# Moving the second head's normalisation of 16 steps from ScalarE to GpSimd in an attention and gated feed-forward kernel

## The chip, the cores and the metric

The kernel runs on one core of a Trainium2 chip. The metric is the time of one execution on the device in microseconds; less is better. A core has five engines that work side by side and wait for each other by semaphores: TensorE (PE in the profile, with PEld for its weight loads), VectorE (DVE), ScalarE (ACT), GpSimd (POOL) and SyncE (SP), whose queue issues most DMAs. TensorE multiplies from SBUF into PSUM. Each engine runs its own instructions strictly in order.

## The reference, cut to what matters

Four batches, eight heads, 768 positions, head width 64. Attention looks back over 96 positions and at 8 global keys, with a distance bias by head; its output goes through a feed-forward part with a convolution of three taps and a gate.

```python
scores = q @ k.T / 8 - slope[h] * dist
scores = where(keep, scores, -1e9)
scores = scores - scores.max(-1)
a = exp(scores)
a = a / (a.sum(-1) + 1e-9)
x = a @ v
h = maximum(x @ w_in, 0)
c = conv3(h, conv_w)
out = (h * sigmoid(c)) @ w_out
```

Changed is who carries out the division in the fifth line, for one of every two heads and for 16 of 96 steps.

## The kernel before, in words

Attention is cut into 32 pairs of heads (4 batches, 2 halves of the sequence, 4 pairs of heads), and each pair into 3 blocks of 128 query rows. One block of one pair is a **step**; there are 96, numbered from 0. For step s, whose pair is m = s // 3, these functions run, each for both heads (j = 0 and 1):

- `scores(s)`, L372: TensorE multiplies queries by the 232 keys in reach (136 for the first block of a sequence), tiles `s` (and `sb`, the second head's, in the first 27 steps). The PSUM tile for the scores has two buffers, so step s + 2 cannot be scored before the exponentials of step s have read theirs.
- `maxima(s)`, L404: VectorE adds the bias table and takes the row's extreme, one instruction a head (L412), into `mm`.
- `exps(s)`, L419: ScalarE takes the exponential with the row sum (L426) into `pbuf`, of which there are three. Below step 32 ScalarE also adds the 1e-9 to both sums (L432).
- `normalise(s)`, L434: VectorE takes the reciprocal of the sums (L438); from step 32 on it first adds the 1e-9 itself (L437). Then each head's exponentials are multiplied by the reciprocal: the first head's by GpSimd (L444), the second head's by ScalarE below step 32 (L442) and by GpSimd from there on.
- `transposes(s)` and `evict(s)`: TensorE transposes `pbuf` into `t` (L452, four matmuls a step), ScalarE copies it out as `pt` (L457).
- After the third step of a pair, `values(m)` multiplies by v into `pv` (L473, 24 matmul rows of the trace a pair), which has one buffer. ScalarE copies it to `xh` (L485), VectorE takes the remainder `xl` = pv - xh (L489). Only then can the next pair's values be written.

The feed-forward part of every half sequence is cut into small items: `mm1` (L507, tiles `h`), `relu` on ScalarE (L517), `conv` (first tap on ScalarE, L555, for the first two halves, then on GpSimd, L557; the other two on VectorE, L558 and L559, tile `c`), the gate (L577), `split` (L610 to L613, tiles `gh` and `gl`) and `mm2` (L622, tile `o`). They are queued and drawn from between the steps. Weights arrive as 64-bit numbers; VectorE takes each piece apart in three instructions (L316, L318, L320, tile `w`), GpSimd makes the high part (L325), VectorE the remainder (L331, tile `wol`). From pair 9 on GpSimd also copies keys and queries (`prep`, L137 and L138, tiles `kk` and `qh`), and VectorE takes their remainders (L141, and L142 into `ql`).

The order on each engine up to step 15 is that of the code. From `HAND = 16` on a scheduler orders all instructions of all engines from its own estimates of their lengths, and so it places every later instruction anew when one instruction changes its engine. `SHARED` is 32.

```python
        if s < HAND:
            scores(s)
...
                normalise(s - 1)
...
        else:
            if hand:
                hand = False
                cur["auto"] = True
                manual.__exit__(None, None, None)
```

Of the kernel before, what the change touches and what calls it, by code (L numbers as in the profile page):

```python
# [36 lines left out]
SHARED = 32  # L37
CHECK_EVERY = 3
HAND = 16
# [28 lines left out]
def fast_path(tc, io):  # L68
# [365 lines left out]
    def normalise(s):  # L434
        pb, c0, n, mm = st_s[s]
        if s >= SHARED:
            V.tensor_scalar(mm[:, 4:6], mm[:, 2:4], 1.0e-9, None, ALU.add)  # L437
        V.reciprocal(mm[:, 6:8], mm[:, 4:6])  # L438
        for j in range(2):
            x, inv = pb[:, j, c0 : c0 + n], mm[:, 6 + j : 7 + j]  # L440
            if j and s < SHARED:
                A.activation(x, x, AF.Copy, scale=inv)  # L442
            else:
                G.tensor_scalar(x, x, inv, 1.0, ALU.mult, ALU.mult)  # L444
# [340 lines left out]
    for s in range(len(steps) + LAG_V + 1):  # L785
        cur["s"] = s
        m, i = steps[s] if s < len(steps) else (len(jobs), -1)
        if s < HAND:
# [14 lines left out]
            if s:  # L803
                normalise(s - 1)
# [17 lines left out]
        else:  # L822
# [20 lines left out]
            if s <= len(steps):  # L843
                normalise(s - 1)
# [222 lines left out]
```

## Time and profile before

| | us |
|---|---|
| median of 3 runs | 446.5 |
| fastest and slowest of them | 445.61 and 447.54 |
| the profiled execution, its own time | 445.31 |
| its span in the profile | 443.5 |
| TensorE busy in the span | 431.2 |
| VectorE busy | 357.2 |
| ScalarE busy | 309.9 |
| GpSimd busy | 221.2 |

The span runs from the first instruction to the last. Durations are of one execution on the hardware; stretches are given in us from the span's start. A mean length stands in ns, times in us. The granted clock is TensorE's, as a share of full speed. Matmuls overlap in the pipeline, so a single matmul's length is longer than the distance to the next. A wait names the instruction that ended it. Step 16 begins at about 43 us, and steps 16 to 31 are normalised until about 108 us.

### The profile page before, as it was taken

What the parts mean: (1) busy time and instruction counts of PE and PEld (TensorE: products, weight loads), DVE (VectorE), ACT (ScalarE), POOL (GpSimd) and SP (SyncE); (2) the same over time, 40 slices, a digit from 0 to 9 for tenths busy, and PEclk for the clock granted to TensorE, in tenths of its full rate; (3) what the DMA queues carried; (4) which work ended last, traced back from release to release, by engine and by line L of the source; (5) the groups of instructions that cost most, each with busy time, mean ns of one, the idle gap of its engine ahead of it and who ended that gap; (6) DMA issues with size and microseconds to landing.
All of it is one profiled execution on the core that took longest, in us unless ns stands there. A gap on an engine that the chain in (4) does not pass through costs nothing.

```text
span 443.5 us, 9050 instructions
## 1 busy us (share of the span) xinstructions
PE 431.2 (97%) x3039; PEld 374.5 (84%) x3039; DVE 357.2 (81%) x935; ACT 309.9 (70%) x839; POOL 221.2 (50%) x307
## 2 busy tenths in 40 slices
PE   8988999799999999999999999999999999999996
PEld 7655778799889988899889988899988998798876
DVE  6899899998999988757998989747999975568700
ACT  4889988789896678546876865665776776755540
POOL 5555334654456786556757744647656841013000
PEclk9999999899999999999999999999999999999999
DMA  6998953141543244442246134423235313980111
GB/s 210 294 255 258 271 184 110 40 163 65 153 128 120 75 136 132 128 125 94 85 128 192 41 107 145 141 102 104 67 119 181 103 48 122 312 295 32 47 49 55
DMA packets 22662, 60.02 MB, mean 135 GB/s; under 512 B 3024, under 2 KB 5584, under 8 KB 22608
## 3 DMA queue, kind: packets, MB, share of 16 engines
q1 hardware_dynamic: 18992, 53.01, 39.2%
q10 hardware_dynamic: 3616, 6.36, 3.9%
q8 instruction: 26, 0.43, 0.4%
q14 instruction: 28, 0.23, 0.2%
HBM read 53.07 MB, written 6.29 MB: 134 GB/s over the span
## 4 chain that ended last, share of the span: by engine, by line
PE 81%; DVE 8%; DMA 6%; ACT 3%; issue 1%; POOL 0%; SPq 0%; DVEq 0%; ACTq 0%
PE o L622 26%; PE h L507 25%; PE pv L473 10%; PE t L452 9%; PE s L395 7%; DMA check<-in_w 3%; PE s L385 1%; PE last L643 1%; DMA out<-ob 1%; DVE w L320 1%; DVE w L318 1%; ACT junkb L350 1%; ACT pbuf L426 1%; DMA rq<-in_qk 1%; PE sb L385 1%
## 5 line engine op out<-in xcount | busy, mean ns | idle before, releaser
L444 POOL TENSOR_SCALAR pbuf<-pbuf,mm 128x232 f32<-128x232 f32 (+1 forms) x160 | 113.3, 718 | 81.0 <-DVE mm L438 49.5
L426 ACT ACTIVATE pbuf<-s,mm 128x232 f32<-128x232 f32 (+1 forms) x165 | 72.1, 442 | 48.3 <-DVE mm L412 34.6
L412 DVE CUSTOM_DVE_ANT_0 s<-s,tab 128x232 f32<-128x232 f32 (+1 forms) x165 | 63.1, 385 | 20.2 <-PE s L395 15.7
L622 PE MATMUL o<-woh,gh 128*128 128x512 f32 x184 | 74.1, 403 | 0.0
L622 PE MATMUL o<-woh,gl 128*128 128x512 f32 x184 | 73.5, 400 | 0.0
L622 PE MATMUL o<-wol,gh 128*128 128x512 f32 x184 | 73.3, 398 | 0.0
L452 PE MATMUL t<-ident,pbuf 128*128 128x128 f32 x384 | 65.4, 279 | 5.4 <-ACT pbuf L442 2.7
L557 POOL TENSOR_SCALAR c<-hbuf,cw 128x382 f32<-128x382 f32 (+1 forms) x48 | 38.6, 807 | 56.5 <-ACT hbuf L517 56.5
L452 PEld LDWEIGHTS t<-ident,pbuf 128*128 128x128 f32 x384 | 46.4, 141 | 20.2 <-ACT pbuf L442 6.4
L457 ACT ACTIVATE pt<-t 128x512 f32<-128x512 f32 x96 | 57.0, 597 | 8.3 <-PE t L452 8.0
L507 PE MATMUL h<-xl,wih 128*128 128x384 f32 x252 | 59.4, 343 | 0.0
L507 PE MATMUL h<-xh,wih 128*128 128x384 f32 x252 | 58.8, 347 | 0.1
L507 PE MATMUL h<-xh,wil 128*128 128x384 f32 x252 | 55.8, 339 | 0.0
L473 PE MATMUL pv<-pt,v 128*64 128x128 f32 (+1 forms) x768 | 50.3, 280 | 0.3 <-DVE xl L489 0.2
L473 PEld LDWEIGHTS pv<-pt,v 128*64 128x64 f32 (+1 forms) x768 | 42.5, 138 | 8.6 <-issue 3.6
L558 DVE SCALAR_TENSOR_TENSOR c<-hbuf,cw,c 128x382 f32<-128x382 f32 (+1 forms) x64 | 44.3, 699 | 4.8 <-POOL c L557 3.7
L559 DVE SCALAR_TENSOR_TENSOR c<-hbuf,cw,c 128x382 f32<-128x382 f32 (+1 forms) x64 | 45.4, 712 | 0.3
L507 PEld LDWEIGHTS h<-xh,wih 128*128 128x128 f32 x252 | 43.2, 190 | 2.1 <-ACT pbuf L426 0.9
L507 PEld LDWEIGHTS h<-xl,wih 128*128 128x128 f32 x252 | 43.9, 189 | 0.7 <-issue 0.7
L507 PEld LDWEIGHTS h<-xh,wil 128*128 128x128 f32 x252 | 44.1, 188 | 0.0
L517 ACT ACTIVATE hbuf<-h 128x384 f32<-128x384 f32 x64 | 31.4, 495 | 13.5 <-PE h L507 12.5
L622 PEld LDWEIGHTS o<-woh,gl 128*128 128x128 f32 x184 | 34.6, 188 | 7.3
(120 smaller groups left out, 856.1 us busy)
## 6 DMA issues: line engine op xcount, KB each, us to landing
v<-in_vv SPq DMA_DIRECT2D x32, 384.0 KB, 3.6
rq<-in_qk SPq DMA_DIRECT2D x23, 384.0 KB, 3.1
wr<-in_w SPq DMA_DIRECT2D x16, 512.0 KB, 5.3
check<-in_w SPq DMA_DIRECT2D x16, 512.0 KB, 4.9
rk<-in_qk SPq DMA_DIRECT2D x12, 504.0 KB, 3.6
out<-ob ACTq DMA_DIRECT2D x23, 256.0 KB, 2.4
rk<-in_qk SPq DMA_DIRECT2D x11, 408.0 KB, 3.6
rq<-in_qk SPq DMA_DIRECT2D x16, 96.0 KB, 5.1
```

The costliest lines, as they stand in the source:

```text
L412: last_ttr[s] = V.tensor_tensor_reduce(out=sp[j][:, c0 : c0 + n], in0=sp[j][:, c0 : c0 + n], in1=tb, scale=-0.125, scalar=3.0e38, op0=ALU. ...
L426: last_exp[s] = A.activation(pb[:, j, c0 : c0 + n], sp[j][:, c0 : c0 + n], AF.Exp, bias=mm[:, j : j + 1], scale=-1.0, accum_out=mm[:, 2 + ...
L444: G.tensor_scalar(x, x, inv, 1.0, ALU.mult, ALU.mult)
L452: T.transpose(pt[:, j, c, :], pb[:, j, c * P : (c + 1) * P], ident)
L457: last_ev[s] = A.activation(sb, st_pt[s], AF.Copy)
L473: T.matmul(pv[m][64 * j : 64 * j + 64, i * P : (i + 1) * P], vt[m][:n, i, c, 64 * j : 64 * j + 64], sb[:n, j, c, :], start=c == 0, stop=c ...
L507: T.matmul(ps[:, :TB], w_[:, k, fs], x_, start=part == 0 and k == 0, stop=part == 2 and k == NK - 1,)
L517: A.activation(half, ps[:, :TB], AF.Relu, scale=0.5)
L557: G.tensor_scalar(c, *tap(1), 1.0, ALU.mult, ALU.mult)
L558: V.scalar_tensor_tensor(c, *tap(0), c, ALU.mult, ALU.add)
L559: V.scalar_tensor_tensor(c, *tap(2), c, ALU.mult, ALU.add)
L622: last = T.matmul(ps, g_[:, f], w_[:, f], start=f == 0 and part == 0, stop=f == NF - 1 and part == 2,)
```

## The change

```diff
         for j in range(2):
             x, inv = pb[:, j, c0 : c0 + n], mm[:, 6 + j : 7 + j]
-            if j and s < SHARED:
+            if j and s < HAND:
                 A.activation(x, x, AF.Copy, scale=inv)
             else:
                 G.tensor_scalar(x, x, inv, 1.0, ALU.mult, ALU.mult)
```

For steps 16 to 31 the second head's exponentials are multiplied by GpSimd, like the first head's. ScalarE goes on adding the 1e-9 up to step 31, and VectorE from step 32 on. Steps 0 to 15 and 32 to 95 have the same instructions as before; from about 48 us on the scheduler orders them anew, until about 245 us.

On GpSimd, steps 16 to 20 (`mm` and the number behind it name the step; `woh` and `wih` are weight casts):

```order
 L325 CAST wih_186<-w3_1_748 128x512
 L444 TENSOR_SCALAR pbuf0_193<-pbuf0_193,mm15_774 128x232
-L444 TENSOR_SCALAR pbuf1_194<-pbuf1_194,mm16_807 128x232
+L444 TENSOR_SCALAR pbuf1_194<-pbuf1_194,mm16_807 128x232 x2
 L325 CAST woh_188<-w4_0_791 128x512
+L444 TENSOR_SCALAR pbuf2_195<-pbuf2_195,mm17_840 128x232 x2
 L325 CAST woh_188<-w4_1_873 128x512
-L444 TENSOR_SCALAR pbuf2_195<-pbuf2_195,mm17_840 128x232
-L444 TENSOR_SCALAR pbuf0_193<-pbuf0_193,mm18_880 128x232
-L444 TENSOR_SCALAR pbuf1_194<-pbuf1_194,mm19_939 128x232
+L444 TENSOR_SCALAR pbuf0_193<-pbuf0_193,mm18_880 128x232 x2
+L444 TENSOR_SCALAR pbuf1_194<-pbuf1_194,mm19_939 128x232 x2
```

Every step's normalisation is now two instructions in a row, and step 17's stands in front of a weight cast that it stood behind.

On VectorE, from step 27's second maximum to the remainder `xl` of pair 6, which the values of pair 7 wait for (`ISA` is the maximum; the row behind each reads its result out):

```order
-L558 SCALAR_TENSOR_TENSOR c0_865<-hbuf_190,cw_185,c0_865 128x382
 L412 ISA s27_1285,mm27_1290<-s27_1285,tab_166 128x136
 L412 ISA mm27_1290 128x1
+L316 TENSOR_SCALAR w7_1_1329<-wr7_1_1065 128x512
+L558 SCALAR_TENSOR_TENSOR c0_865<-hbuf_190,cw_185,c0_865 128x382
 L438 RECIPROCAL mm26_1261<-mm26_1261 128x2
-L316 TENSOR_SCALAR w7_1_1329<-wr7_1_1065 128x512
-L331 TENSOR_TENSOR wol_189<-w6_1_1199,woh_188 128x512
 L412 ISA s28_1342,mm28_1347<-s28_1342,tab_166 128x232
 L412 ISA mm28_1347 128x1
 L489 TENSOR_TENSOR xl6_1222<-pv6_1171,xh6_1221 128x384
```

The tap L558 has moved from in front of the maximum to behind it, and the weight remainder L331 from in front of `xl6` to behind it.

On VectorE, around step 40's maxima, which step 42's scores wait for:

```order
-L412 ISA s40_1963,mm40_1968<-s40_1963,tab_166 128x232
-L412 ISA mm40_1968 128x1
 L613 TENSOR_TENSOR gl0_4_1947<-hbuf_190,gh0_4_1946 128x1024
 L412 ISA s40_1963,mm40_1968<-s40_1963,tab_166 128x232
 L412 ISA mm40_1968 128x1
+L489 TENSOR_TENSOR xl11_1974<-pv11_1917,xh11_1973 128x384
 L437 TENSOR_SCALAR mm39_1908<-mm39_1908 128x2
+L412 ISA s40_1963,mm40_1968<-s40_1963,tab_166 128x232
+L412 ISA mm40_1968 128x1
 L412 ISA s41_2018,mm41_2023<-s41_2018,tab_166 128x232
```

The remainder `xl11` and the addition L437 now stand in front of step 40's second maximum; counted from the start, only L437 is new ahead of it, since `xl11` stood further forward before.

## Rows read from the trace of the kernel before

**Rows 1.** The waits, TensorE, 50 to 400 us: total us, times, longest us.

```profile
PE s L395 <- ACT pbuf L426: 2.1, 1, 2.1
PE pv L473 <- DVE xl L489: 0.2, 1, 0.2
```

**Rows 2.** Busy time by stretch, the columns in the first line.

```profile
core 0: us, PE busy (x) PEld busy (x) DVE busy (x) ACT busy (x) POOL busy (x), PEclk, DMA share, GB/s
...
70.00:80.00 10.00, 10.00 (x78) 8.95 (x77) 9.94 (x27) 9.72 (x32) 6.30 (x7) 1.00 0.39 122
80.00:90.00 10.00, 7.70 (x57) 6.87 (x57) 9.94 (x24) 7.13 (x21) 5.72 (x6) 0.83 0.24 72
90.00:140.00 50.00, 50.00 (x368) 45.48 (x368) 47.71 (x110) 43.34 (x110) 24.63 (x29) 1.00 0.40 126
...
45.00:107.00 62.00, 59.70 (x422) 51.76 (x422) 58.33 (x150) 54.02 (x159) 28.60 (x34) 0.97 0.45 140
```

**Rows 3.** The chain of waits, 75 to 145 us: start, us, what.

```profile
82.38 0.53 DVE c L558
...
83.65 0.60 DVE wol L331
85.10 2.61 PE pv L473 x24
```

**Rows 4.** The timeline, 76 to 92 us: start, length, instruction [idle before].

```profile
81.49 0.60 PE L452 MATMUL t<-ident,pbuf 128*128 128x128 f32 x4
...
82.83 0.29 DVE L412 CUSTOM_DVE_ANT_0 s<-s,tab 128x136 f32<-128x136 f32 x1
...
84.15 0.38 PE L395 MATMUL s<-kk,qh 128*128 128x232 f32 x1 [2.06 <-ACT pbuf L426]
...
84.49 0.55 DVE L489 TENSOR_TENSOR xl<-pv,xh 128x384 fp32r<-128x384 f32 x1
...
84.96 1.30 DVE L559 SCALAR_TENSOR_TENSOR c<-hbuf,cw,c 128x382 f32<-128x382 f32 x1
84.98 0.86 POOL L137 CAST kk<-rk 128x816 fp32r<-128x816 f32 x1 [0.49 <-PE s L395]
...
85.10 2.61 PE L473 MATMUL pv<-pt,v 128*64 128x128 f32 x24 [0.24 <-DVE xl L489]
...
87.64 1.11 PE L452 MATMUL t<-ident,pbuf 128*128 128x128 f32 x4
```

**Rows 5.** The timeline, 130 to 142 us.

```profile
139.52 0.39 DVE L412 CUSTOM_DVE_ANT_0 s<-s,tab 128x232 f32<-128x232 f32 x1
...
139.72 1.54 PE L473 MATMUL pv<-pt,v 128*64 128x128 f32 x24
...
139.84 0.67 DVE L437 TENSOR_SCALAR mm<-mm 128x2 f32<-128x2 f32 x1
...
141.19 0.19 PEld L395 LDWEIGHTS s<-kk,qh 128*128 128x128 f32 x1 [0.17 <-ACT pbuf L426]
```

**Rows 6.** The source lines L442 and L444: ns min/median/max, first and last start us.

```profile
L442 ACT ACTIVATE pbuf<-pbuf,mm x32: 392/477/519, 10.3 to 107.5; 128x232 f32<-128x232 f32 x25, 128x136 f32<-128x136 f32 x7
...
L444 POOL TENSOR_SCALAR pbuf<-pbuf,mm x160: 373/459/2478, 9.5 to 370.8; 128x232 f32<-128x232 f32 x135, 128x136 f32<-128x136 f32 x25
```

**Rows 7.** The waits, VectorE, 50 to 145 us.

```profile
DVE s L412 <- PE s L395: 1.3, 1, 1.3
DVE sb L412 <- PE sb L385: 0.7, 1, 0.7
DVE c L558 <- ACT c L555: 0.7, 2, 0.5
```

**Rows 8.** The timeline, step 23's normalisation on GpSimd and its transposes.

```profile
74.51 1.09 POOL L444 TENSOR_SCALAR pbuf<-pbuf,mm 128x232 f32<-128x232 f32 x1 [3.19 <-DVE mm L438]
...
76.96 0.60 PE L452 MATMUL t<-ident,pbuf 128*128 128x128 f32 x4
```

**Rows 9.** The source line L559, then its group in 45 to 107 us (busy us, mean ns).

```profile
L559 DVE SCALAR_TENSOR_TENSOR c<-hbuf,cw,c x64: 592/618/1297, 51.4 to 410.6; 128x382 f32<-128x382 f32 x32, 128x386 f32<-128x386 f32 x32
...
L559 DVE SCALAR_TENSOR_TENSOR c<-hbuf,cw,c 128x382 f32<-128x382 f32 x8 | 5.5, 690 | 0.0
```

## The prediction, made before the changed kernel had run

> **What bounds the kernel now.** The first view is the list of waits of TensorE (PE). From 50 to 400 us it waited twice: 2.1 us in front of a score matmul and 0.2 us in front of the value matmuls that follow [rows 1]. After that it runs back to back, so whatever moves the moment at which TensorE gets past its last shortage of input moves the end by as much, and nothing else does.
>
> The second view is busy time by stretch [rows 2]. VectorE (DVE) is busy 9.94 of 10 us from 70 to 80 and from 80 to 90, and 47.71 of 50 from 90 to 140. TensorE reads as fully busy in all of them but 80 to 90, where it has 7.70 of 10 at a mean granted clock of 0.83. So two engines are full at once, and the chain of waits says which one leads: before 85.10 it is made of VectorE instructions, after 85.10 of matmuls [rows 3]. The timeline shows the handover [rows 4]. The maximum of step 27's second head starts on VectorE at 82.83; ScalarE's exponential of it lets the scores of step 29 begin at 84.15, after 2.06 us without a matmul. The remainder xl of pair 6 starts on VectorE at 84.49, and the values of pair 7 wait for it until 85.10. TensorE then runs at the lower of its two clock levels (1.2 GHz) for a while: the 24 value matmuls take 2.61 us where the same 24 take 1.54 at 139.72, and four transposes take 1.11 us where four took 0.60 just before [rows 4, 5]. A mean clock of 0.83 over 10 us is 1.7 us lost. Everything that could be won here is 2.06 + 0.24 + 1.7 = 4.0 us.
>
> One later place matters. At 141.19 TensorE's weight load for step 42's scores was held 0.17 us by the exponentials of step 40, whose second maximum began on VectorE at 139.52 [rows 5]. There TensorE arrives with nothing to spare, so a TensorE that came earlier would wait for VectorE.
>
> **The change, part by part.** *ScalarE* loses 16 instructions of 0.477 us, 7.6 us in all [rows 6]. It is not on the chain where it leads, so this is worth nothing by itself. What it can give is earlier inputs to VectorE, which waited 0.7 us in all for ScalarE's first convolution tap [rows 7]. I take 0.5 of it.
>
> *GpSimd* gets 16 instructions more, 16 x 0.459 = 7.3 us undisturbed [rows 6]. It has them free: 28.60 of 62 us busy from 45 to 107 [rows 2]. Both heads of a step now stand in line there, so a step is ready one instruction later than its first head. The transposes would feel it. The smallest distance I find in steps 16 to 31 is step 23's: normalised at 75.60 (74.51 + 1.09), transposed from 76.96, 1.36 us [rows 8]. One more instruction of 0.46 to 1.09 us fits, and in the new order step 23's transposes stand behind the four score matmuls of step 27. Cost taken: nothing. Without that cover it would be some 0.5 us, once.
>
> *VectorE* does the same work, but beside a busier GpSimd. The rows show that the two hold each other up. A convolution tap that takes 0.592 us at best took 1.30 when a GpSimd cast of 0.86 began 0.02 us after it [rows 4, 9]. In 45 to 107 us the eight instructions of L559 average 0.690 against that best of 0.592, 0.8 us lost on 4.7, 17% [rows 9]. GpSimd was then busy 28.60 us [rows 2]; 7.3 more is a quarter more, and a quarter of 17% is 4%, on all of VectorE's 58.33 us 2.4 us. That is too much, since the maxima read their scores from PSUM and part of the work is on one operand, and since a normalising instruction (0.459) holds VectorE for less than the cast above; I take half, 1.2. The ends are nothing (none meets such an instruction) and 7.3 us (each holds VectorE for its whole length); 1.2 is nearer the low one because the 17% is a measured rate.
>
> The Trainium skill (SBUF — State Buffer, "Who interferes with whom") speaks against the change here: a VectorE instruction with two SBUF inputs and a GpSimd instruction that reads SBUF share a port, and whichever starts first keeps the other out for its whole length. The long tap agrees with that. An estimate by the rule, with half a GpSimd instruction lost at each of 16, would be 3.7 us in place of 1.2, and the sum below 448.7 in place of 446.2; the second rival is this case, priced from rows.
>
> *The order* is written by a scheduler, so it moves too. In front of step 27's second maximum one tap (0.53 us on the chain) now stands behind it; in front of xl of pair 6, one weight remainder L331 (0.60) [rows 3]. TensorE's own work in front of step 29's scores, of pair 7's values and of step 42's scores is the same before and after. So the wait at 84.15 is met about 0.5 us sooner, less the share of the 1.2 us that falls before it (11 of 16 steps, 0.8), plus the 0.5 from ScalarE. It shrinks by a few tenths and does not go; the lower clock is likely to follow it again. Further on, six transposes (0.15 us each at most) that stood before step 32's scores stand behind them, which brings these 0.7 us nearer. VectorE had waited 1.3 us for them [rows 7], and with both shifts I let that wait go whole. In front of step 40's second maximum VectorE's work is again the same but for one two-column addition (L437), 0.67 us where it stands now [rows 5] and taken as 0.4.
>
> **The sum**, at step 42's scores, where TensorE last has nothing to spare: +1.2 (held up) + 0.4 (L437) - 0.5 (ScalarE) - 1.3 (wait for step 32) = -0.2 us on VectorE. TensorE's own path is earlier by about as much, so the later of the two gives -0.2 to -0.4; I write -0.3. The profiled execution took 445.3 us (span 443.5), so 445.0 there. The median of the runs shown is 446.5, 1.2 above it, so on the median **446.2 us**. With the loss anywhere from 0 to 2.4 us and the waits gone or kept, this case reaches from 444.6 to 448.2: at the top 2.4 + 0.4 of loss against 1.1 of waits won back, at the bottom TensorE's path earlier by the 0.5 and by part of the lower clock.
>
> **Rivals.** *The stall goes.* If the extra GpSimd work meets VectorE seldom, the loss is 0, the 0.7 us wait for a score and the 0.5 go, and 1.3 more at step 32: -2.5 + 0.1, 444.1 us. If VectorE also keeps ahead at step 40, all of 4.0 us comes back: 442.5. For it: the new order removes work ahead of exactly the two late VectorE instructions, and a shorter wait might leave the clock up. Against it: VectorE is idle only 2.3 us from 90 to 140 and 0.06 in each of the two stretches before [rows 2], so it has hardly anything to speed up with.
>
> *VectorE is held longer.* Place: steps 16 to 31, each time a second normalising instruction starts just ahead of a tap, a weight piece or a remainder. Price: 0.25 us each is 4.0 us; with 0.4 for L437 and less the 1.2 that the waits give back (0.5 of ScalarE, half of step 32's) it is +3.2, 449.7 us. It decides from about 0.2 us each (3.2 + 0.4 - 1.2 = 2.4 us). For it: the cast's 0.7 us on one tap. Against it: the measured rate of the taps, and the normalising instruction's shortness.
>
> *The transposes become late.* If GpSimd runs its casts for the queries and keys in front of a pair, a transposition waits 0.5 to 1 us, and with a fall of the clock (1.7) the kernel is some 2.4 us slower, 448.9. Against it is the 1.36 us above, and that in steps 32 and later both heads are already there without TensorE waiting [rows 1].
>
> **How the numbers follow.** A measurement of this kernel can tell about 0.5%, 2.2 us, from no change. Forecast 0.60, all within that bound. The stall goes: 0.22, faster. VectorE held longer 0.15 and late transposes 0.03, slower. Hence faster 0.22, same 0.60, slower 0.18. The range from 442.8 to 449.2 takes in the forecast's own, most of the first rival and the near part of the other two.
>
> **What would show it.** In the profile after: ScalarE's L442 with 16 instructions and GpSimd's L444 with 176; VectorE busy as much as now from 50 to 140, with its two-operand groups up by about 1.2 us in all; a wait of TensorE near 84 us of 1.3 to 2.1 us, for the exponentials or for xl; a mean clock below 1.00 in that stretch. The forecast is wrong if TensorE shows no wait there and the clock stays up, if the two-operand groups grow by over 3 us, or if TensorE has a new wait for GpSimd's normalising.

## The result, and the profile after

The change made the kernel slower: 450.5 us median of 7 runs (448.9 to 452.3) against 446.0 for the kernel before (445.0 to 447.5, 7 runs). The ratio is 1.0108, with a 95% interval of 1.0081 to 1.0135. The forecast was 446.2 us with a range up to 449.2, and the median lies 1.3 us above that upper end. The profiled execution has a span of 448.6 us, 5.1 more than before.

The instructions are what the change says: ScalarE keeps 16 of 32, GpSimd has 176 in place of 160 [rows 6]. The source rows of the two lines:

```profile
L442 ACT ACTIVATE pbuf<-pbuf,mm x16: 394/476/480, 10.3 to 46.0; 128x232 f32<-128x232 f32 x12, 128x136 f32<-128x136 f32 x4
...
L444 POOL TENSOR_SCALAR pbuf<-pbuf,mm x176: 372/459/2568, 9.5 to 375.6; 128x232 f32<-128x232 f32 x148, 128x136 f32<-128x136 f32 x28
```

The list of TensorE's waits from 50 to 400 us answers [rows 1]:

```profile
PE s L395 <- ACT pbuf L426: 3.5, 2, 2.0
PE h L507 <- ACT xh L485: 1.5, 1, 1.5
PE h L507 <- ACT hbuf L517: 1.1, 1, 1.1
PE t L452 <- POOL pbuf L444: 0.7, 1, 0.7
```

That is 6.8 us where there were 2.3. The wait of before is still there, 2.05 us in front of step 29's scores, now at 85.09. Four others are new, at 76.98 (1.12), 82.43 (1.51), 119.87 (1.41, step 36's scores) and 128.49 (0.74, step 35's transposes).

Busy time by stretch after the change (the columns are those of [rows 2]):

```profile
70.00:80.00 10.00, 8.88 (x57) 8.09 (x57) 9.94 (x22) 7.33 (x23) 6.20 (x9) 1.00 0.36 111
80.00:90.00 10.00, 6.45 (x40) 5.32 (x39) 9.91 (x26) 5.00 (x13) 5.60 (x7) 0.74 0.14 42
90.00:110.00 20.00, 20.00 (x139) 19.10 (x139) 15.80 (x35) 14.86 (x40) 9.13 (x12) 0.96 0.34 105
...
110.00:130.00 20.00, 17.85 (x135) 14.82 (x134) 19.40 (x54) 17.34 (x46) 9.32 (x13) 1.00 0.40 132
```

and the two of before that [rows 2] do not have apart:

```profile
90.00:110.00 20.00, 20.00 (x158) 19.26 (x156) 18.55 (x42) 18.39 (x51) 9.12 (x11) 1.00 0.30 101
110.00:130.00 20.00, 20.00 (x148) 17.02 (x145) 19.24 (x51) 17.64 (x45) 8.79 (x14) 1.00 0.44 127
```

Read the three stretches from the top. From 70 to 90 TensorE now runs dry three times. The mean granted clock of 0.74 and then 0.96 loses 2.6 + 0.8 = 3.4 us to the lower level (1.2 GHz), 1.7 more than before. From 90 to 110 TensorE reads as full, but VectorE, full before, is idle for 4.2 us of 20 (1.45 before). From 110 to 130 TensorE idles for 2.15 us; the chain of waits below shows what it stood behind. The waits (+4.5) and the clock (+1.7) make 6.2 us, 1.1 more than the span grew. TensorE's busy time in the whole span is 431.3 us where it was 431.2, although more of it ran at the lower level; so the rest came back in the length of its own work, and which matmuls it was is not known.

The further 1.7 us of the clock is not in every run. Two of the seven runs of the change, 448.9 and 449.9 us, had a mean granted clock of 0.996 like the profiled run of before; the profiled one had 0.992.

What VectorE waited for is in its own list, 50 to 145 us (before: [rows 7]):

```profile
DVE hbuf L610 <- ACT c L577: 2.0, 2, 1.6
DVE s L412 <- ACT gh L612: 1.3, 1, 1.3
DVE mm L438 <- ACT mm L432: 0.9, 1, 0.9
```

In that stretch of before none of the three was in the list. The longest shows how such a wait comes about. The input of the tanh L577 was ready at about 92.8 us, when the last tap L559 ended. In ScalarE's new queue it stands behind the eviction of h1_0, and TensorE had that only at 95.19. So VectorE idled 1.60 us until 96.45.

The chain of waits, 88 to 150 us, shows what follows. Before, the line that sums it by source names TensorE alone:

```profile
by line: PE h L507 46.8%; PE o L622 18.1%; PE t L452 12.5%; PE pv L473 11.8%; PE s L395 11.2%
```

After, the chain leaves TensorE at 106.4 us, goes over VectorE and ScalarE for 22 us, with only the 0.72 us of step 36's scores between, and comes back at 128.5 (start, us, what):

```profile
106.19 0.23 PE t L452 x2
...
106.44 0.60 ACT pt L457
...
110.18 1.21 DVE kk L141
...
114.01 0.87 DVE ql L142
...
118.84 0.99 ACT pbuf L426 x4
...
119.87 0.72 PE s L395 x4
...
127.98 0.47 POOL pbuf L444
...
128.49 0.44 PE t L452 x2
```

### The profile page after: what moved, and what is told of

Same layout as the page of the kernel before. It is cut to its first block, busy times and chain, and to the rows that moved or that the text cites. A ratio compares the mean times of both kernels' runs of the same rounds, so it can differ in the third digit from the quotient of the medians.

```text
span 448.6 us, 9076 instructions
## 1 busy us (share of the span) xinstructions
PE 431.3 (96%) x3039; PEld 374.7 (84%) x3039; DVE 360.7 (80%) x935; ACT 304.8 (68%) x823; POOL 228.8 (51%) x323
## 4 chain that ended last, share of the span: by engine, by line
PE 81%; DVE 12%; ACT 4%; issue 1%; DMA 1%; POOL 1%; DVEq 0%; ACTq 0%; POOLq 0%
PE o L622 27%; PE h L507 26%; PE pv L473 9%; PE t L452 8%; PE s L395 7%; ACT pbuf L426 2%; DVE s L412 2%; DVE c L558 1%; PE last L643 1%; DVE c L559 1%; PE s L385 1%; DVE kk L141 1%; DVE w L318 1%; DVE w L320 1%; DVE w L316 1%
## 5 line engine op out<-in xcount | busy, mean ns | idle before, releaser
L444 POOL TENSOR_SCALAR pbuf<-pbuf,mm 128x232 f32<-128x232 f32 (+1 forms) x176 | 123.1, 711 | 86.4 <-DVE mm L438 47.3
L426 ACT ACTIVATE pbuf<-s,mm 128x232 f32<-128x232 f32 (+1 forms) x165 | 72.1, 442 | 56.7 <-DVE mm L412 35.0
L507 PE MATMUL h<-xh,wih 128*128 128x384 f32 x252 | 60.6, 351 | 2.6 <-ACT xh L485 1.5
L558 DVE SCALAR_TENSOR_TENSOR c<-hbuf,cw,c 128x382 f32<-128x382 f32 (+1 forms) x64 | 44.5, 702 | 5.1 <-POOL c L557 4.7
L559 DVE SCALAR_TENSOR_TENSOR c<-hbuf,cw,c 128x382 f32<-128x382 f32 (+1 forms) x64 | 44.4, 696 | 0.5
L622 PEld LDWEIGHTS o<-woh,gh 128*128 128x128 f32 x184 | 34.7, 189 | 6.6 <-issue 0.7
```

The lines of the kernel that those rows point to most:

```text
L426: last_exp[s] = A.activation(pb[:, j, c0 : c0 + n], sp[j][:, c0 : c0 + n], AF.Exp, bias=mm[:, j : j + 1], scale=-1.0, accum_out=mm[:, 2 + ...
L507: T.matmul(ps[:, :TB], w_[:, k, fs], x_, start=part == 0 and k == 0, stop=part == 2 and k == NK - 1,)
L558: V.scalar_tensor_tensor(c, *tap(0), c, ALU.mult, ALU.add)
L559: V.scalar_tensor_tensor(c, *tap(2), c, ALU.mult, ALU.add)
L622: last = T.matmul(ps, g_[:, f], w_[:, f], start=f == 0 and part == 0, stop=f == NF - 1 and part == 2,)
```

## The experiments

Two theories were open. **Order:** the moved work costs little, and the new order of all queues that the scheduler wrote around it costs the time. **Work:** GpSimd's 16 further operations hold VectorE up, or are late. To part them, a table of numbers was put into the kernel that fixes every engine's queue from step 16 on; the instructions are otherwise traced as they were:

```diff
+ORDER = {
+    "PE": "10 11 12 13 ...
...
-                es.enter_context(tc.manual_schedule(engines={mybir.EngineType.PE}))
...
+    for seq in ORDER.values():
+        seq = [real[int(n)] for n in seq.split()]
...
+        for a, z in zip(seq, seq[1:]):
+            tc.add_manual_dep(
+                z, a.name,
...
```

**1. The change's engines, the old order.** The changed kernel, with the table of before; each moved instruction stands behind its step's first head on GpSimd.

> The change's engines (GpSimd normalises the second head of steps 16 to 31 too) in the order of before: a table fixes each engine's queue from step 16 on to the one of the kernel before, and each of the 16 normalisations that moved stands on GpSimd right behind that of its step's first head. Theory A (the new order that the scheduler wrote costs the time, the moved work itself little): about 446, between 445 and 447.5 (ratio to before 0.998 to 1.004), with TensorE's wait near 84 us as in before and none of the four new ones near 77, 82, 120 and 128 us. Theory B (the moved work costs it: GpSimd holds VectorE up, and the second head's exponentials are ready later): 449 to 451 as the change (ratio 1.007 to 1.012), with new waits of TensorE for ScalarE or VectorE behind step 27 in spite of the old order.

**2. The old engines, the new order.** The kernel before, with the table of the change.

> The reverse: the engines of before (ScalarE normalises the second head of steps 16 to 31) in the order that the scheduler wrote for the change, by the same kind of table; each of the 16 normalisations stands on ScalarE near the neighbours that it had in before. Theory A (order): 449 to 451 (ratio 1.007 to 1.013), with TensorE's waits near 77, 82 and 85 us as after the change. Theory B (work): 445 to 447 (ratio 0.998 to 1.003), with one wait near 84 us as before. In between, 447.5 to 449, both would have a share.

Measured: 446.8 us, ratio 1.0042 (1.0016 to 1.0068) for the first, and 449.4, 1.0063 (1.0036 to 1.0089) for the second. Their excesses, 0.42% and 0.63%, add up to 1.05%, where the change has 1.08%. So both theories have a part. The ratio compares all runs and is not the quotient of the medians; the kernel before, run beside them, had a median of 446.4. At equal mean clock the first is 1 to 2 us slower than before (446.2 to 446.9 against 444.6 to 445.0 at 0.995 and 0.996), the second 2 to 4 (446.5 and 446.7 against 443.8 to 445.2 at 0.999 and 1.000, 448.1 to 449.1 against 444.6 to 445.0 at 0.996). The two intervals overlap, so that the order's part is the larger, some 2.8 us of 4.7, rests on the waits and on the table of lateness under experiments 3 and 4. TensorE's waits in the first (lines stand 9 higher in these two kernels, where the table is at the top; L404 is L395, L435 is L426):

```profile
PE s L404 <- ACT pbuf L435: 3.2, 1, 3.2
```

It is the one wait of before, 1.1 us longer. None of the four new ones came. In the second they are all there, though ScalarE does the work as it always did:

```profile
PE s L404 <- ACT pbuf L435: 3.3, 2, 1.9
PE h L515 <- ACT hbuf L525: 0.9, 1, 0.9
PE h L515 <- ACT xh L493: 0.8, 1, 0.8
PE t L461 <- POOL pbuf L453: 0.8, 1, 0.8
```

The 1.1 us of the first has its place: step 27's second maximum starts 1.22 us later than before [rows 4], that of step 22 only 0.02.

```profile
84.05 0.29 DVE L421 CUSTOM_DVE_ANT_0 s<-s,tab 128x136 f32<-128x136 f32 x1
```

**3 and 4. Where in the new order the time goes.** The change's engines, with the queues of the two orders joined at a point that both have reached: old up to 104 us and then new, and new up to 105.5 us and then old.

> The change's engines; every queue in the old order up to what had begun by 104 us in the profile of before (step 32's scores and before), in the new order from there on. The change with the old order all through gave 446.8 (ratio 1.0042), the change itself 450.5 (1.0108). If the new order loses its time in the first part (TensorE runs dry near 77, 82 and 85 us, and is at half clock for 3.4 us more): about 446.8 (1.002 to 1.006). If it loses it behind that (the new waits near 120 and 128 us, VectorE idle near 95 and 105 us): 449.5 to 450.5 (1.008 to 1.012). If both have a share: about 448.5.

> The reverse of the run before it: the change's engines, every queue in the new order up to what had begun by 105.5 us in the profile of after, in the old order from there on. If the loss sits in the first part: 449.5 to 450.5 (ratio 1.008 to 1.012). If it sits behind that: about 446.8 (1.002 to 1.006). If both have a share: about 448.5; the two ratios' excesses over 1.0042 should then add up to about that of the change, 0.0066.

Measured: old then new 452.1 us, 1.0129 (1.0099 to 1.0160, 6 runs); new then old 447.8, 1.0064 (1.0036 to 1.0091). By the ratios the second part of the new order costs more than the first. Above the 1.0042 of experiment 1 they make 0.0087 and 0.0022 (the latter within its noise), 0.0109 together where the change has 0.0066, so they do not add up as the expectation had asked. But all six runs of old then new had a mean clock of 0.992 or less, where the kernel before spread from 0.989 to 1.000. At 0.991 and 0.992 the change took 450.3 to 452.1 us and old then new 450.7 to 452.4: it is not shown to be slower than the change.

The profiled runs have such falls of the clock too, in front of the place where the orders part (near 48 us). In old then new TensorE had lost 2.9 us before step 16, and in new then old and in experiment 2 some 1.6 us by step 17, at a granted clock of 0.66 from 39 to 44 us. The rows show that stretch in the kernel before and in experiment 2: length, TensorE's busy time, granted clock, DMA:

```profile
39.00:44.00 5.00, 4.59 (x40) 1.00 0.78 207
...
39.00:44.00 5.00, 4.59 (x32) 0.66 0.82 210
```

The lateness that arose behind it can be read from two starts on VectorE, the second maxima of step 17 and of step 95, the last:

| | step 17 | step 95 | later than before | of it behind step 17 |
|---|---|---|---|---|
| before | 46.62 | 365.36 | | |
| change's engines, old order | 46.64 | 366.36 | 1.00 | 0.98 |
| old engines, new order | 48.23 | 370.18 | 4.82 | 3.21 |
| old then new | 49.56 | 372.56 | 7.20 | 4.26 |
| new then old | 48.18 | 368.73 | 3.37 | 1.81 |
| the change | 46.65 | 370.48 | 5.12 | 5.09 |

One run each, so these are no intervals. In them the order costs 3.2 us and the work 1.0; 0.9 of the change's 5.1 is in neither, and only the change lost 3.4 us to the lower clock between 84 and 93 us, the others 1.7. Above the old order the two parts of the new one make 3.28 and 0.83, 4.11 together, which is what the change has (5.09 - 0.98). So here they do add up, and most of the order's cost lies behind 104 us. The waits say where the parts lie:

```profile
PE s L395 <- ACT pbuf L426: 4.6, 2, 3.2
PE t L452 <- POOL pbuf L444: 0.7, 1, 0.7
```

for old then new (the 3.2 is the old wait near 88; 1.41 and 0.73 come at 121.82 and 130.45, as after the change), and for new then old

```profile
PE s L395 <- ACT pbuf L426: 2.0, 1, 2.0
PE h L507 <- ACT xh L485: 1.4, 1, 1.4
PE h L507 <- ACT hbuf L517: 1.1, 1, 1.1
PE pv L473 <- ACT pt L457: 0.8, 1, 0.8
```

where the first three lie before 87 us and the last is a wait at 119.76 that neither order had. So the old order behind 104 us brings most of the time back, and what is left, 0.2% by the ratio, is not clear of the noise.

**5. Is it one wait of VectorE?** The change in its own order, but for the tanh:

```diff
 ScalarE's queue of the change, near 93 us
 L432 mm28
+L577 c0
 L426 s29
 L517 h1_0
-L577 c0
```

> The change in its own order, but for one instruction: on ScalarE the tanh of the last quarter of c0 (L577) stands two places earlier, ahead of the first exponential of step 29 and of the eviction L517 of h1_0, which in the profile of after held it until TensorE had h1_0 ready (95.2 us), though its input was there at 92.8; VectorE then idled 1.60 us for it. Theory A (VectorE's idle time at 92 to 96 us is what starves TensorE behind 110 us): VectorE's wait falls to under 0.5 us, TensorE's waits near 120 and 128 us (1.41 and 0.74) shrink to under 0.7 together, time 448.5 to 449.5 (ratio 1.006 to 1.009). Theory B (the loss behind 104 us lies in the order there, whatever VectorE did before): waits near 120 and 128 us stay above 1.5, time 450 to 451 (1.009 to 1.012).

Measured: 450.2 us, 1.0087 (1.0056 to 1.0118), a time in the range of theory B, a ratio in that of theory A, and not to be told from the change. The waits decide. Two rows of VectorE's list, and two of TensorE's:

```profile
DVE s L412 <- ACT gh L612: 1.7, 1, 1.7
...
DVE hbuf L610 <- ACT c L577: 0.4, 1, 0.4
```

```profile
PE s L395 <- ACT pbuf L426: 3.4, 2, 2.0
...
PE t L452 <- POOL pbuf L444: 0.9, 1, 0.9
```

The 1.6 us for the tanh became 0.4. The next wait in VectorE's queue took part of it, 1.7 where it was 1.3, and TensorE's near 120 and 128 us stayed, 1.4 and 0.9. My theory A, that this one wait is what starves TensorE later, is wrong. Other neighbours in the queue were not tried one by one.

**6. Is the 1.22 us GpSimd's working time?** Experiment 1, with each moved operation cut to 8 columns:

```diff
-            x, inv = pb[:, j, c0 : c0 + n], mm[:, 6 + j : 7 + j]
+            x, inv = pb[:, j, c0 : c0 + (8 if j and HAND <= s < SHARED else n)], mm[:, 6 + j : 7 + j]
```

> The change's engines in the old order (the run that gave 446.8, ratio 1.0042, and step 27's second maximum 1.22 us later), but GpSimd normalises only 8 of the second head's columns in steps 16 to 31, which leaves the rest of them out. If the 1.2 us come from GpSimd holding VectorE up while it works: step 27's second maximum is back within 0.4 us of before, ratio 0.998 to 1.002. If they come from ScalarE's queue or from the waits that the moved instruction brings, whatever its length: the maximum stays about 1 us late, ratio 1.003 to 1.006.

The time, 2913 us, says nothing of this. With columns left as they are, the kernel's flag sends it on to its general path (L980 to L999 fill the trace behind the stretch shown here), which computes everything again. The stretch before that can still be read. The second maxima of steps 22 and 27, of before for step 22 (step 27's is in [rows 4], 82.83) and then of this run:

```profile
64.04 0.41 DVE L412 CUSTOM_DVE_ANT_0 sb<-sb,tab 128x232 f32<-128x232 f32 x1 [0.75 <-PE sb L385]
```

```profile
66.94 0.41 DVE L412 CUSTOM_DVE_ANT_0 sb<-sb,tab 128x232 f32<-128x232 f32 x1 [0.75 <-PE sb L385]
...
85.88 0.29 DVE L412 CUSTOM_DVE_ANT_0 s<-s,tab 128x136 f32<-128x136 f32 x1
```

Here too the profiled run was 2.90 us late from the start; step 27 is 3.05 late, so 0.15 of it arose on the way, against 1.22 with whole operations. The same 16 instructions with the same waits, only shorter, make VectorE late by an eighth of that.

Shorter instructions also have the exponentials ready sooner, so VectorE might have waited less. It did not. Between these two maxima, step 17's and step 27's, it runs the same instructions in the same order in before, in experiment 1 and here. The rows give the stretch, its length and VectorE's busy time, in this order:

```profile
46.62:82.82 36.20, 34.46 (x92) 1.00 0.54 159
46.64:84.04 37.40, 35.68 (x92) 1.00 0.49 153
49.52:85.87 36.35, 34.33 (x92) 1.00 0.51 154
```

VectorE is idle 1.74, 1.72 and 2.02 us. The whole 1.22 us of experiment 1 are longer instructions of VectorE, and with 8 columns they are as short as before. It is GpSimd's working time. In the new order it takes more: the same stretch of experiment 2 (ScalarE normalises) and of the change (GpSimd does), which have one order, differ by 1.58 us of VectorE's busy time.

```profile
48.23:84.15 35.92, 34.53 (x91) 1.00 0.46 146
46.65:83.19 36.54, 36.11 (x91) 1.00 0.54 155
```

**7 to 10. A better order?** If TensorE's wait near 84 us hangs on three places in the queues, they can be mended, in both kernels. Runs 7 and 8 (before, change) have the first three moves, runs 9 and 10 the other two besides:

```diff
 VectorE, from 79.9 us of before
 L412 s27, first head
+L412 s27, second head
 L141 kk10
+L489 xl6
 L320 w7_0
 L558 c0
-L412 s27, second head
...
 L412 s28, second head
+L489 xl7
...
 ScalarE
 L485 xh6
+L426 s27, both heads
 L577 c0
 L457 pt24
-L426 s27, both heads
...
 TensorE
 L395 s28
+L452 t24
 L507 h1_2, h1_0
-L452 t24
```

> The kernel before in its own order, but for three places: on VectorE the second maximum of step 27 stands right behind the first (ahead of L141's key plane, L320 and L558), and xl6 (L489) right behind the key plane; on ScalarE the two exponentials of step 27 stand ahead of the tanh L577 and the eviction of step 24. It prices the stall near 84 us (2.06 us of waiting and 3.4 us at half clock, of which 1.7 are lost). If the stall is worth what the rows say and nothing takes its place: 442 to 444 (ratio 0.991 to 0.996). If VectorE, busy 9.9 us of 10 there, only passes the wait on to a later step: 445.5 to 447 (0.998 to 1.002).

> The same three moves on the change's engines in the old order (the run that gave 446.8, 1.0042). If GpSimd's longer work only made step 27's second maximum 1.2 us later and so lengthened the stall near 84 us, then the moves take that cost away too: 442 to 444.5, within 1 us of the repaired kernel with the old engines. If GpSimd holds VectorE up elsewhere as well, it stays 1 to 2 us behind that kernel.

> The kernel before with the three moves of the run that gave 445.1 (ratio 0.9991), where TensorE's wait near 84 us fell from 2.06 to 0.74 but one of 1.60 came at 91.1 us (weighted sums of step 24 to 26, behind xl7), and two more moves: the transposes of step 24 right behind step 28's scores (the exponentials of step 27 waited for them, 1.40 us, as they overwrite what is transposed), and xl7 (L489) on VectorE right behind step 28's second maximum, not behind 3.4 us of other work. If these waits hang on the order alone: both gone, 442 to 444 (ratio 0.992 to 0.997), faster than both kernels. If VectorE as a whole is the bound there: the waits come back at a later place, 444.5 to 446 (0.997 to 1.001).

> The same five moves on the change's engines in the old order (without moves 1.0042, with three 1.0048). If the change can be worth something in a good order: at or below the kernel of the run before this one, 0.992 to 0.998. If GpSimd's longer work costs VectorE 1 to 2 us here whatever the order: 1 to 2 us more than that kernel, 0.996 to 1.003.

| | before | change's engines |
|---|---|---|
| old order | 1 | 1.0042 (1.0016 to 1.0068) |
| three moves | 0.9991 (0.9961 to 1.0020) | 1.0048 (1.0023 to 1.0073) |
| five moves | 0.9993 (0.9965 to 1.0022) | 1.0034 (1.0007 to 1.0061) |

No version beats the kernel before, and in all three rows the change's engines cost 0.4 to 0.6%. TensorE's waits with five moves on the kernel before:

```profile
PE pv L473 <- ACT pt L457: 1.3, 1, 1.3
PE h L507 <- ACT xh L485: 0.7, 1, 0.7
```

The wait near 84 us is gone, and the clock is 1.00 throughout the stretch. TensorE's matmuls start 2.59 us sooner from step 32 to 35 (step 34's scores at 107.49, 110.07 before). Then it waits 1.33 us at 115.72 for an eviction, and from step 36 on 0.96 us of the gain is left. VectorE, busy 9.9 of 10 us from 70 to 100 in this run too, was not made any faster by the moves. By their ratios both runs on the kernel before met their second expectation. The runs with the change's engines stayed 2.2 and 1.2 us behind them by the medians, which was the second expectation there too.

**11 and 12. Fewer operations moved.** The plain test, with the scheduler's own order:

```diff
-            if j and s < SHARED:
+            if j and s < 24:
```

and the same with 28.

> The kernel before with the second head's normalisation moved for steps 24 to 31 only (the test reads s < 24), in the order that the scheduler writes for it: TensorE's queue is the old one up to its 480th instruction (near 82 us), not up to its 326th as with the change. If the time follows the number of operations moved (half of the change's): 1.003 to 1.006. If it follows the order that comes out: any value from 0.996 to 1.012, with no reason to lie halfway; TensorE's waits in its profile then tell the sign.

> The same for steps 28 to 31 only (s < 28): TensorE's queue is the old one up to its 580th instruction (near 102 us). By number, a quarter of the change: 1.001 to 1.003. By the order: a value that need not lie between before and the run from step 24; as the new order of the change lost most of its time behind 104 us, a loss of 0.004 and more would say that a few moved operations are enough to bring such an order about.

Measured: from step 24 (8 moved) 1.0066 (1.0037 to 1.0095), from step 28 (4 moved) 1.0073 (1.0044 to 1.0103). Sixteen cost 1.08%, eight 0.66, four 0.73. The intervals of these three overlap, but four cost more than a quarter of the change would be (0.3%), so the time does not follow their number. With four moved, TensorE's queue and its wait near 84 us are those of before, and new waits came at 116.84, 120.92 and 135.32, behind step 33, where the order had changed:

```profile
PE s L395 <- ACT pbuf L426: 2.1, 1, 2.1
PE t L452 <- ACT pt L457: 0.6, 1, 0.6
PE pv L473 <- ACT pt L457: 0.5, 1, 0.5
PE t L452 <- POOL pbuf L444: 0.4, 1, 0.4
```

With eight, one of 2.7 us in front of pair 7's values came at 84.72, for xl6:

```profile
PE pv L473 <- DVE xl L489: 2.7, 1, 2.7
```

That wait of before for the exponentials is gone; 1.1 and 0.8 us came at 117.47 and 126.13 besides.

Not run: the kernel before with its own order fixed by the table. What the table itself costs can be seen in the mended kernels, which have the old order up to the moves: there every second maximum of steps 16 to 26 starts within 0.03 us of before. Behind the moves it is not shown apart.

## Why the prediction was wrong, point by point

**The order is the step that failed.** The prediction read the new order at three places where TensorE was already short of input, found that "TensorE's own work in front of step 29's scores, of pair 7's values and of step 42's scores is the same before and after", and let the new order give 1.3 us back at step 32. In the sum the order stood as 1.3 us won, less 0.4 for L437, and as nothing lost elsewhere. Experiment 2 has that order alone, at +0.63%, some 2.8 us lost. What stands in front of those three matmuls is indeed the same in sum, but it stands elsewhere. TensorE's queue shows it (the difference of the two programs near step 25; `h_5` is a group of the feed-forward layer, `s_1211` step 25's scores, `pv_1171` pair 6's values):

```
 L385 MATMUL sb_1151<-rk_927,rq_928 128x136
+L473 MATMUL pv_1171<-pt_1099,v_933 64x128 x4
+L473 MATMUL pv_1171<-pt_999,v_933 64x128 x4
+L473 MATMUL pv_1171<-pt_1047,v_933 64x128 x4
+L385 MATMUL s_1211<-rk_927,rq_928 128x232
 L507 MATMUL h_5_1135<-xh_490,wih 128x384
```

These had stood behind that group. TensorE then ran dry at 76.98 and 82.43, places where it had never waited and which I therefore had not looked at. Experiment 2 shows that the order brings these waits; that it is this one move is not tested. The same holds behind 104 us, for 119.87 and 128.49: the prediction treated TensorE as safe between steps 29 and 42, since the list of waits was empty there. An empty list says that nothing is late in that order; it does not say by how much.

**VectorE held up: right.** The term was +1.2 us, with bounds of 0 and 7.3. In the old order step 27's second maximum is 1.22 us late, all of it longer VectorE instructions, and 0.15 with the operations cut to 8 columns. Up to there the prediction had counted only 0.8 of it; that the total came so close is in part luck, as it was half of an estimate of 2.4. The Trainium skill's rule (SBUF — State Buffer, "Who interferes with whom") gave an estimate of 3.7. The direction agrees with these runs; a price of half an operation each does not, at least up to step 27, and no run shows what a single meeting costs. The prediction says that the long tap agrees with the rule. Its rows agree only in that the two engines hold each other up: the tap's record begins 0.02 us before the cast's, and yet it was the tap that took longer, while the cast had its shortest time, 0.86.

**What was to come back did not.** Against that 1.2 the prediction set 0.5 us from ScalarE's relief and 1.3 from step 32. With the order held still, the change's engines lost 0.42%, 1.9 us by the ratio and 0.9 by the profiled span. There VectorE's wait for ScalarE's first tap did fall from 0.7 to 0.2 us, but another of 0.8 for scores came, where 0.2 had stood:

```profile
DVE sb L421 <- PE s L394: 0.8, 1, 0.8
...
DVE c L566 <- ACT c L563: 0.2, 1, 0.2
```

So from step 17 to 27 it idled as long as before. In the new order VectorE's waits for step 32's and other late scores did shrink, from 1.3 to 0.6 us in that row of its list, but the three rows shown above, 4.2 us, took their place. The sum had counted a wait as gone without asking what VectorE would stand in front of next.

**The wait near 84 us: half right.** It stayed, and the lower clock followed, as forecast. It was to shrink by a few tenths; it is 2.05 us where it was 2.06, with two new ones in front of it, and in the profiled run the clock took 3.4 us where it had taken 1.7.

**The rivals.** "VectorE is held longer" gave 449.7 us, near the result, by a mechanism that was not at work in that size: its 0.25 us an operation would be 2.8 for the 11 up to step 27, and the runs show 1.2 in the old order and 1.6 in the new. "The transposes become late" has its sign in the profile, a wait of 0.74 us for GpSimd's L444, which the prediction had named as a sign of being wrong. But it is at step 35, whose second head GpSimd normalised before the change as well, and experiment 2 has it (0.8) with the old engines. A rival in which the order by itself costs the time was missing.

## What to carry to other kernels

Where a scheduler writes the order, a change of a few instructions is two changes; four moved normalisations out of 96, with the order that came with them, were enough for 0.7%. Price them apart by fixing the old order under the new instructions and the new order under the old ones, before looking for a cause in the hardware. To judge a new order from the trace of the old one, look at how close each input of the leading engine came to being late, not only at the places where it was late.

## What the runs showed that I had not expected

Runs of one program differ by the time that TensorE spends at the lower level, and they do so in steps. Beside experiments 1 and 2 the kernel before ran 22 times: 443.8 to 445.2 us in the six runs with a mean granted clock of 0.999 or 1.000, 444.6 to 445.0 in the three at 0.996, and 446.2 to 448.4 in the thirteen at 0.991 or 0.992. In the traces of all runs but experiment 6, each stretch at the lower level lost 1.7 or 3.4 us; the two mended kernels with the old engines lost none. By the profile of before, 0.996 is the one loss near 85 us, so the six runs above it can have had none there, though no trace of such a run was kept. From the first group to the last the medians rise by 2.4 us, less than the two losses of 1.7 that the means tell of. So a single profiled run does not tell on which step a kernel stands, and steps of this size are as large as the part of the change that GpSimd's work explains.
